# A three-layer fp32 network on one core: the scheduler's slacks, begin, look-ahead and transfer latency set to other values, and 28 leading idle transposes in place of 18

## The chip, the cores and the metric

The kernel runs on one core of one Trainium2 chip. The metric is the device time of one execution in microseconds. Before the change it is 800.46 us, the median of three runs (800.13 to 802.74 us). One more execution was profiled: it took 801.54 us, of which 799.8 us lie between its first and its last instruction. All rows below are of that execution.

Engines are named as in the profile: PE is the matrix engine (PEld its weight loads), DVE the vector engine, ACT the scalar engine, POOL the GpSimd engine, SP the engine that issues the DMAs.

## The reference

The program computes three layers in a row, all in fp32:

```python
# attention over a memory of 32 slots, 4 images x 8 heads, 576 positions, head size 64
a = exp(phi - max(phi, positions)); a = a / (sum(a, positions) + 1e-9)
k_m, v_m = einsum('bhsm,bhsd->bhmd', a, k), einsum('bhsm,bhsd->bhmd', a, v)
attn = softmax(q @ k_m^T / 8, slots)
x = (attn @ v_m) as 2304 tokens x 512
# layer 2
h = x @ w_in            # 512 -> 2048
g = maximum(0.01 * h, h)
x = g @ w_out           # 2048 -> 512
# layer 3
out = ((x @ w_a) * (x @ w_b)) @ w_out2   # 512 -> 1536, 1536 -> 512
```

## The kernel before, in words

**Arithmetic.** A product of two fp32 matrices is made of three passes of a faster number format: both factors are split into a high and a low part, and high x high, high x low and low x high are added up in PSUM (`PASSES`). The weights arrive as 64-bit words. Each weight tile is converted before use: two ACT operations (`high`, `low`, lines 460 and 463), then `clamp` (L467 on DVE, L392 on POOL), `shift` (L471), `join` (L475) and `add` (L478), and for most weights a copy to the high part (L405 on ACT, L407 on DVE) and a subtraction for the low part (L484 on DVE, L388 on POOL).

**Stages of the beginning.** For each image b and each half g of the heads, `kv_part` loads phi, k and v. It takes the maximum on DVE (L540) and the exponential on ACT (L541), transposes on PE (tiles `ta`, `tz`, L554 and L557) and copies the result back (`en`). PE multiplies it with k and v (tile `km`, L571), DVE normalises (`kvn`, L580), and PE transposes once more (`kvt`, L588). Two pairs of copies lead from there to `kd` and `vm`. `sc_both` then multiplies q with `kd` (tile `sc`, L632). `sc_part` is the softmax of these scores: on DVE a transpose (L654), the maximum (L662), the subtraction (L663), on ACT the exponential (L664), on DVE the sum and its reciprocal (L667 to L669), the product (L672) and a transpose back (L673). ACT copies the high part (`ahi`, L405), and DVE (L678) or POOL (L388) makes the low part (`alo`).

**Layer 2.** The values of the memory are first multiplied with `w_in` (`vw_unit`, L704; high and low part `vwh` and `vwl`, L714). `h_unit` (L757) then multiplies `ahi` and `alo` with `vwh` and `vwl`; `y_unit` (L796) multiplies the result `g` with `w_out`. There are four chunks of `w_in` and `w_out`, eight pieces of tokens (two for each image), and for each piece four blocks of h. Layer 3 (`ab_unit` L1008, `left_unit` L1062, `o_unit` L1102, `o_part` L1217) works through 12 chunks of its weights twice.

**What sets the order.** Nothing runs in the order in which the code is written. Each step is recorded as an `Op` with an engine (or several to choose from), a cost in microseconds and what it reads and writes. `Program.order` then plays the whole program through in a planned time and gives every step an engine, a place in that engine's queue and a buffer. Among the steps that are ready it takes the one with the earliest due time `o.late`. The due times come from `urgency`: the large matrix steps (those with a `pos`) have target times, which begin at `START` and add up their costs, and every other step is due so much earlier as its followers need, less its own `slack` from the table `SLACK`. `LEAD` says how many places ahead of the first one still missing a large matrix step may be taken. `LAT_DMA` is the planned delay between a transfer's end and its reader. The engines then execute their queues strictly in the order that came out.

SP's queue too is written in this order: it issues 323 transfers one after the other, and each begins when its buffer is free.

**Names in the change.** `warm` (L424) is the first work of PE: transposes of the identity matrix whose result nobody reads.

Of the kernel before, what the change touches and what calls it, by code (L numbers as in the profile page):

```python
# [52 lines left out]

PRE = 4
TURN = 0.15
SEVEN = 8
LEAD = 12
SLACK = {'phi0': 0.0, ('kv0', 0): 1.0, ('kv0', 1): 0.0, 'kvr0': 3.0, ('q0', 0): 0.0, ('q0', 1): 0.0, ('win0', 0): 5.37, ('win0', 1): 5.37, ('wout0', 0): 8.13, ('wout0', 1): 8.13, 'win': 4.9, 'wout': 4.64, 'wa': 23.6, 'wb': -0.15, 'wout2': 16.8, ('sc', 0, 0): 6.2, ('sc', 0, 1): 3.3, ('sc', 1, 0): 8.05, ('sc', 1, 1): 6.75, ('sc', 2, 0): 11.99, ('sc', 2, 1): 9.96, ('vw', 0, 0): 19.04, ('vw', 0, 1): 7.99, ('vw', 0, 2): 9.35, ('vw', 1, 0): -0.31, ('vw', 1, 1): 19.18, ('vw', 1, 2): 8.18}
START = 17.4
BIAS = 0.5  # L60
POOL_BIAS = 0.8
LAT, LAT_SAME, LAT_DMA = 0.4, 0.1, 1.0
OVER = {'PE': 0.0, 'ACT': 0.0, 'DVE': 0.0, 'POOL': 0.0, 'DMA': 0.0}
BLOCKED = 0.0
DMA_RATE, DMA_FIRST = 355e3, 0.0
SPARE = {'PE': 1.0, 'ACT': 1.03, 'DVE': 1.03, 'POOL': 1.03, 'DMA': 1.2}


# [20 lines left out]
def c_dma(nbytes):  # L89
    return max(0.6, nbytes / DMA_RATE)  # L90
# [15 lines left out]
class Program:  # L106
# [13 lines left out]
    def op(self, eng, cost, fn, r=(), w=(), tiles=(), pos=None, ahead=60.0, keep=0, slack=0.0, soon=False):  # L120
        o = Op()
        port = isinstance(eng, Port)
        o.costs = {e: (c - OVER[e]) * SPARE[e] for e, c in (eng if isinstance(eng, dict) else {eng: cost}).items()}
        eng = next(iter(o.costs))
        cost = o.costs[eng]
        o.eng, o.cost, o.fn, o.tiles, o.pos, o.seq, o.ahead, o.keep = eng, cost, fn, tuple(tiles), pos, len(self.ops), ahead, keep
        o.slack, o.soon = slack, soon
        o.port = port
        o.before, o.after = set(), []
        for x in r:  # L130
            if x in self.writer:
                o.before.add(self.writer[x])
        for x in w:
            if x in self.writer:
                o.before.add(self.writer[x])
            o.before.update(self.readers.pop(x, ()))
        for x in r:
            self.readers.setdefault(x, set()).add(o)
        for x in w:
            self.writer[x] = o  # L140
        o.before.discard(o)
        for x in o.before:
            x.after.append(o)
        self.ops.append(o)
        return o
# [20 lines left out]
    def order(self, target):  # L166
# [59 lines left out]
        while left:  # L226
# [5 lines left out]
            for e in ready:  # L232
                if at[e] > now + 1e-9:
                    continue
                for o in ready[e]:
                    if o.dep > now + 1e-9:
                        continue
                    if o.pos is not None and index[o.seq] > nth + LEAD:
                        continue
# [54 lines left out]
    def run(self, make, rounds=6):  # L294
        main = [o for o in self.ops if o.pos is not None]
        main.sort(key=lambda o: o.pos)
        target, t = {}, START
        for o in main:
# [35 lines left out]
def tile_mem_attention__leaky_mlp__bilinear_mlp(  # L334
# [29 lines left out]
    op, tile_of = pr.op, pr.tile  # L364
# [55 lines left out]
    tile_of(("warm",), "y", [P])  # L420

    def warm(T):
        for _ in range(18):
            nc.tensor.transpose(T["warm",], ident, ident)  # L424

    op("PE", 5.0, warm, tiles=[("warm",)], ahead=1e12)

# [11 lines left out]
    def weight(kind, c, k, after=()):  # L441
# [51 lines left out]
        op(Port({"DVE": 0.68}), 0, join, r=[raw], w=[a], tiles=[raw, cv], ahead=any_time)  # L493
        slack = SLACK[(kind + "0", k // 2) if first else kind]
        op(Port({"DVE": 0.62, "POOL": 2.45}), 0, add, r=[("l", key)], w=[a], tiles=[cv], ahead=any_time, slack=slack if kind == "win" else 0.0)
# [17 lines left out]
    def kv_part(b, g):  # L513
# [4 lines left out]
        if b == 0:  # L518
            tile_of(phi, "slot", [1, S])
            op("DMA", c_dma(P * S * 4), lambda T: nc.sync.dma_start(T[phi], phiT[b, :, g:g + 1, :]), w=[("e", b, g)], tiles=[phi], slack=SLACK["phi0"])  # L520
        elif g == 0:
# [9 lines left out]
        for i, k in enumerate(kvt):  # L531
            tile_of(k, "slot", [2, 512])
            op("DMA", c_dma(P * 4096), lambda T, i=i, k=k: nc.sync.dma_start(T[k], kv[b, g, :, 2 * i:2 * i + 2, :]), w=[k], tiles=[k], keep=6 if b else 0, slack=0 if b else SLACK["kv0", g])
        if g == 0:
            tile_of(rest, "slot", [2, 512], parts=64)
            op("DMA", c_dma(64 * 4096), lambda T: nc.sync.dma_start(T[rest], kv_rest[b]), w=[rest], tiles=[rest], keep=6 if b else 0, slack=0 if b else SLACK["kvr0"])

# [68 lines left out]
    def q_load(b, g):  # L606
# [5 lines left out]
        for x in range(2):  # L612
            q, cols = ("q", b, g, x), piece(x)
            n = cols.stop - cols.start
            tile_of(q, "slot", [2, n])
            op("DMA", c_dma(P * n * 8), lambda T, q=q, cols=cols: nc.sync.dma_start(T[q], qT[b, g, :, :, cols]), w=[q], tiles=[q], slack=SLACK["q0", x])

    def sc_both(b, x):
# [17 lines left out]

        op("PE", 4 * n / 2.4e3 + TURN, s_sc, r=[*qs, *(("kd", b % 2, g) for g in range(2))], w=scs, tiles=[*qs, *scs])
        for i in range(2):
            sc_part(b, i, x)

    def sc_part(b, g, x):
# [24 lines left out]
        def s_sum(T):  # L666
# [11 lines left out]
            lambda T, e: engines[e].tensor_tensor(T[alo][:, g, cols], T[at], T[ahi][:, g, cols].bitcast(F32), op=ALU.subtract),  # L678
            r=[at, kh], w=[kl], tiles=[at, ahi, alo], slack=SLACK["sc", min(b, 2), x],
        )  # L680
# [8 lines left out]
    def vw_unit(c, b, x, n):  # L689
# [9 lines left out]
        def prod(T):  # L699
# [6 lines left out]
        op(  # L706
            "PE", TURN + 4 * n / 2.4e3, prod, r=[("a", k[1:]) for k in ws] + [("vm", b, g) for g in range(2)], w=os, tiles=[*os, *ws],
            ahead=15.0,
# [364 lines left out]
    def by_seven(s, c):  # L1073
        return s == 1 and c < SEVEN

# [126 lines left out]
    def o_part(q, x, nth, pos):  # L1202
# [18 lines left out]
        def acc(i):  # L1221
            return ("osum", i)

        def part(T, i):
            return T[acc(i)][:, x, :]
# [12 lines left out]
        if q == 0:  # L1238
            op({"ACT": c_act(NB2), "DVE": c_dve(NB2)}, 0, lambda T, e: copy(e, part(T, i), T[o]), r=[o], w=[tok(i)], tiles=[o, acc(i)])
            return  # L1240
        last = q == SEVEN // 2 - 1
        op("DVE", 0.69, lambda T: nc.vector.tensor_tensor(part(T, i), T[o], part(T, i), op=ALU.add), r=[o], w=[tok(i)], tiles=[o, acc(i)])
# [116 lines left out]
```

## Time and profile before

| | us |
|---|---|
| median of three runs (lowest, highest) | 800.46 (800.13, 802.74) |
| the profiled execution | 801.54 |
| its span, first to last instruction | 799.8 |
| PE busy in the span | 775.5 (97%) |
| DVE, ACT, POOL busy | 615.9, 372.6, 119.9 |

[...] A row of a timeline gives start, duration, engine, line, operation, output and inputs, shape and number of the instructions that were merged into it. In brackets stands how long the engine was idle just before, and what it waited for.

### The profile page before, as it was taken

What the parts mean: (1) busy time and instruction counts of PE and PEld (TensorE: products, weight loads), DVE (VectorE), ACT (ScalarE), POOL (GpSimd) and SP (SyncE); (2) the same over time, 40 slices, a digit from 0 to 9 for tenths busy, and PEclk for the clock granted to TensorE, in tenths of its full rate; (3) what the DMA queues carried; (4) which work ended last, traced back from release to release, by engine and by line L of the source; (5) the groups of instructions that cost most, each with busy time, mean ns of one, the idle gap of its engine ahead of it and who ended that gap; (6) DMA issues with size and microseconds to landing.
All of it is one profiled execution on the core that took longest, in us unless ns stands there. A gap on an engine that the chain in (4) does not pass through costs nothing. (4 is left out here: it accounts for less than half of the span.)

```text
span 799.8 us, 12802 instructions
## 1 busy us (share of the span) xinstructions
PE 775.5 (97%) x4754; PEld 661.9 (83%) x4754; DVE 615.9 (77%) x1179; ACT 372.6 (47%) x810; POOL 119.9 (15%) x176
## 2 busy tenths in 40 slices
PE   6689999999999999999999999999999999999998
PEld 4367788989898889899988888888888888888886
DVE  5797798689868986676756988998864666798855
ACT  4557676757444754444435635444321154232210
POOL 0132051014003500010000302131210100024100
PEclk6679999999999999999999999999999999999999
DMA  9974211367143722033878854666487988777402
GB/s 331 387 233 143 91 70 54 99 203 246 46 145 111 273 65 79 1 107 109 304 262 306 277 190 167 227 206 212 166 286 287 310 267 286 233 229 239 150 1 105
DMA packets 56558, 149.99 MB, mean 188 GB/s; under 512 B 7216, under 2 KB 22576, under 8 KB 56496
## 3 DMA queue, kind: packets, MB, share of 16 engines
q1 hardware_dynamic: 56496, 149.18, 54.8%
q8 instruction: 37, 0.61, 0.3%
q14 instruction: 25, 0.20, 0.1%
HBM read 103.55 MB, written 45.61 MB: 187 GB/s over the span
## 5 line engine op out<-in xcount | busy, mean ns | idle before, releaser
L796 PE MATMUL y<-g,wout 128*128 128x320 f32 (+1 forms) x1152 | 216.1, 340 | 1.0 <-DVE wout L484 0.8
L796 PEld LDWEIGHTS y<-g,wout 128*128 128x128 f32 x1152 | 187.5, 190 | 23.1 <-issue 6.3
L1008 PE MATMUL abx<-yb_T,wo 128*128 128x512 f32 x432 | 110.2, 390 | 0.0
L1102 PE MATMUL o<-p,wout 128*128 128x512 f32 x384 | 94.9, 390 | 0.0
L1008 PEld LDWEIGHTS abx<-yb_T,wo 128*128 128x128 f32 x432 | 80.2, 188 | 16.1 <-ACT t L1019 0.2
L1019 ACT COPY t<-abx 128x512 f32<-128x512 f32 x72 | 42.1, 585 | 101.9 <-PE abx L1008 101.7
L722 ACT ACTIVATE g<-h 128x320 fp32r<-128x320 f32 (+1 forms) x128 | 52.5, 411 | 70.8 <-PE h L757 66.9
L1102 PEld LDWEIGHTS o<-p,wout 128*128 128x128 f32 x384 | 72.0, 188 | 15.3 <-DVE osum L1115 0.4
L757 PE MATMUL h<-ahi,vwh 128*128 128x320 f32 (+1 forms) x256 | 78.5, 307 | 2.7 <-ACT ahi L405 1.8
L757 PE MATMUL h<-alo,vwh 128*128 128x320 f32 (+1 forms) x256 | 76.6, 299 | 1.3 <-POOL alo L388 1.0
L757 PE MATMUL h<-ahi,vwl 128*128 128x320 f32 (+1 forms) x256 | 76.3, 298 | 0.0
L811 DVE TENSOR_TENSOR acc<-y,acc 128x320 f32<-128x320 f32 (+1 forms) x72 | 40.1, 556 | 36.7 <-PE y L796 36.3
L773 DVE TENSOR_TENSOR g<-t,g 128x256 fp32r<-128x256 f32 (+1 forms) x112 | 52.5, 473 | 17.8 <-ACT t L722 17.0
L757 PEld LDWEIGHTS h<-ahi,vwh 128*128 128x128 f32 x256 | 48.9, 191 | 11.6 <-issue 4.5
L722 ACT ACTIVATE t<-h 128x320 f32<-128x320 f32 (+1 forms) x128 | 52.3, 409 | 0.2
L757 PEld LDWEIGHTS h<-alo,vwh 128*128 128x128 f32 x256 | 49.0, 191 | 2.6 <-POOL alo L388 1.6
L757 PEld LDWEIGHTS h<-ahi,vwl 128*128 128x128 f32 x256 | 49.0, 191 | 0.0
L1016 DVE TENSOR_TENSOR t<-abz,t 128x512 f32<-128x512 f32 x48 | 33.0, 687 | 20.0 <-ACT t L1019 10.9
L1115 DVE TENSOR_TENSOR oacc<-o,oacc 128x512 f32<-128x512 f32 x40 | 27.5, 688 | 14.8 <-PE o L1102 13.9
L405 ACT CAST p<-t 128x512 fp32r<-128x512 f32 x31 | 19.2, 620 | 39.9 <-DVE t L1040 26.1
L1008 PE MATMUL abx<-yb_B,wo 128*128 128x512 f32 x144 | 36.9, 392 | 0.0
L1008 PE MATMUL abz<-yb_B,wo 128*128 128x512 f32 x144 | 36.7, 390 | 0.0
(311 smaller groups left out, 1348.2 us busy)
## 6 DMA issues: line engine op xcount, KB each, us to landing
k_wo<-wo SPq DMA_DIRECT2D x32, 512.0 KB, 5.0
wo<-k_wo SPq DMA_DIRECT2D x32, 512.0 KB, 4.6
raw_wout<-in_w_out_dram SPq DMA_DIRECT2D x24, 512.0 KB, 5.6
raw_win<-in_w_in_dram SPq DMA_DIRECT2D x16, 512.0 KB, 5.5
kv<-in_kv_dram SPq DMA_DIRECT2D x16, 512.0 KB, 10.6
k_yb_T<-yb_T SPq DMA_DIRECT2D x8, 512.0 KB, 7.2
raw_wa<-in_w_a_dram SPq DMA_DIRECT2D x8, 512.0 KB, 4.1
raw_wb<-in_w_b_dram SPq DMA_DIRECT2D x8, 512.0 KB, 4.6
```

Source lines behind the costliest of these rows:

```text
L405: nc.scalar.copy(dst, src)
L722: nc.scalar.activation(dst, src, AF.Prelu, alpha=0.01)
L757: nc.tensor.matmul(T[o], T[w[u]][:, k, fs], T[a[v]][:, k, cols], start=(k == 0 and i == 0), stop=(k == 1 and i == 2))
L773: lambda T, e: engines[e].tensor_tensor(T[g][:, i, 1, to], T[t], T[g][:, i, 0, to].bitcast(F32), op=ALU.subtract),
L796: nc.tensor.matmul(T[o], w[:, u, es], T[g][:, j, v, :], start=(f == 0 and p == 0), stop=(f == 3 and p == 2))
L811: "DVE", c_dve(m), lambda T: nc.vector.tensor_tensor(T[acc][:, i, :], T[o], T[acc][:, i, :], op=ALU.add),
L1008: nc.tensor.matmul(T[o], T[w][:, which, u, k * P:(k + 1) * P], T[ys[v]][:, k, :], start=first and k == 0 and x == 0, stop=k == 1 and x == ...
L1016: op("DVE", 0.69, lambda T: nc.vector.tensor_tensor(T[to], T[o], T[x], op=ALU.add), r=[o, x], w=[to], tiles=[o, x, to])
L1019: op("ACT", 0.59, lambda T: nc.scalar.copy(T[t], T[X]), r=[X], w=[t], tiles=[X, t])
L1102: nc.tensor.matmul(T[o], T[w][:, u, es], T[g][:, at, v, :], start=(x == 0 and k == 0), stop=(x == 1 and k == 2))
L1115: "DVE", c_dve(size), lambda T: nc.vector.tensor_tensor(T[acc][:, i, :], T[o], T[acc][:, i, :], op=ALU.add),
```

## The change

Only numbers change. The slacks are other ones for nearly every kind of step. `START` is 10.21 and not 17.4, so that all due times move forward against the transfers and conversions. `LEAD` is 9 and not 12, `LAT_DMA` 1.12 and not 1.0. The idle transposes are 28, and their planned cost is 0.28 us for each (7.84 us, before 5.0 us). Two names without effect (`DMA_FIRST`, the type of zeros in `OVER`) go too. The computation and the number of large matrix instructions stay the same.

```diff
+WARM = 28
-LEAD = 12
-SLACK = {'phi0': 0.0, ('kv0', 0): 1.0, ('kv0', 1): 0.0, 'kvr0': 3.0, ...
+LEAD = 9
+SLACK = {'phi0': -0.83, ('kv0', 0): 1.64, ('kv0', 1): -4.32, 'kvr0': 4.67, ...
-START = 17.4
+START = 10.21
-LAT, LAT_SAME, LAT_DMA = 0.4, 0.1, 1.0
+LAT, LAT_SAME, LAT_DMA = 0.4, 0.1, 1.12
...
-        for _ in range(18):
+        for _ in range(WARM):
             nc.tensor.transpose(T["warm",], ident, ident)

-    op("PE", 5.0, warm, tiles=[("warm",)], ahead=1e12)
+    op("PE", 0.28 * WARM, warm, tiles=[("warm",)], ahead=1e12)
```

The new lines are one further down: L588 is L589 in the changed program.

PE, image 0: the products `km` of both halves and the transposes `kvt` behind them. Before:

```order
L571 MATMUL km_0_189<-kvr_156,en_0_163 32x128 x4
L588 MATMUL kvt_0_221<-ident,kvn_0_217 128x128 x2
L571 MATMUL km_1_228<-kv_1_0_185,en_1_175 32x128 x8
L571 MATMUL km_1_228<-kv_1_1_211,en_1_175 32x128 x8
L571 MATMUL km_1_228<-kvr_156,en_1_175 32x128 x4
L588 MATMUL kvt_1_255<-ident,kvn_1_253 128x128 x2
```

and changed:

```order
L572 MATMUL km_0_197<-kvr_128,en_0_175 32x128 x4
L572 MATMUL km_1_233<-kv_1_0_192,en_1_180 32x128 x8
L572 MATMUL km_1_233<-kv_1_1_219,en_1_180 32x128 x8
L572 MATMUL km_1_233<-kvr_128,en_1_180 32x128 x4
L589 MATMUL kvt_0_256<-ident,kvn_0_229 128x128 x2
L589 MATMUL kvt_1_265<-ident,kvn_1_259 128x128 x2
```

The second `km` no longer stands behind the first `kvt`, which waits for DVE's `kvn`. Behind these rows, PE in both programs makes the first half of `vw` of image 0. Before, the second half and image 1's `ta` and `tz` follow and then the scores `sc` of image 0; now the scores come at once, then `ta` and `tz`, then the second half.

DVE, the softmax of image 0's first scores (`sm_0_0` and `sm_1_0` are its two halves, `mx` their maxima). Before:

```order
L407 COPY en_0_309<-ta_0_298 128x512
L714 TENSOR_TENSOR vwl_0_281<-vw_0_1_0_284,vwh_0_278 128x256
L714 TENSOR_TENSOR vwl_0_281<-vw_0_1_1_285,vwh_0_278 128x256
L467 TENSOR_SCALAR cv_wout_0_311<-cv_wout_0_311 128x512
L467 TENSOR_SCALAR cv_wout_1_315<-cv_wout_1_315 128x512
L467 TENSOR_SCALAR cv_wout_2_323<-cv_wout_2_323 128x512
L471 TENSOR_SCALAR cv_wout_0_311<-cv_wout_0_311 128x512
L471 TENSOR_SCALAR cv_wout_1_315<-cv_wout_1_315 128x512
L654 STREAM_TRANSPOSE sm_0_0_356<-sc_0_0_338 128x320
L654 STREAM_TRANSPOSE sm_1_0_359<-sc_1_0_339 128x320
L662 TENSOR_REDUCE mx_0_10_81<-sm_0_0_356 128x10
L662 TENSOR_REDUCE mx_0_10_83<-sm_1_0_359 128x10
```

and changed:

```order
L541 TENSOR_REDUCE kst_0_79<-phi_254 128x1
L541 TENSOR_REDUCE kst_1_80<-phi_254 128x1
L715 TENSOR_TENSOR vwl_0_291<-vw_0_0_0_275,vwh_0_288 128x256
L715 TENSOR_TENSOR vwl_0_291<-vw_0_0_1_276,vwh_0_288 128x256
L545 TENSOR_SCALAR kst_0_79<-kst_0_79 128x1
L546 RECIPROCAL kst_0_79<-kst_0_79 128x1
L655 STREAM_TRANSPOSE sm_0_0_315<-sc_0_0_294 128x320
L655 STREAM_TRANSPOSE sm_1_0_324<-sc_1_0_295 128x320
L663 TENSOR_REDUCE mx_0_10_81<-sm_0_0_315 128x10
L663 TENSOR_REDUCE mx_0_10_83<-sm_1_0_324 128x10
L664 TENSOR_TENSOR sm_0_0_315<-sm_0_0_315,mx_0_10_81 128x320
L664 TENSOR_TENSOR sm_1_0_324<-sm_1_0_324,mx_0_10_83 128x320
```

The softmax now stands ahead of all of DVE's work on the weight `w_out`, which moves behind it, and ahead of the second half of `vwl`. The two copies of `ta` to `en` of image 1 are ACT's now.

DVE, the end of that softmax (`at`) and the step to its low part `alo`. Before:

```order
L673 STREAM_TRANSPOSE at_0_0_387<-sm_0_0_356 128x320
L673 STREAM_TRANSPOSE at_1_0_412<-sm_1_0_359 128x320
L471 TENSOR_SCALAR cv_wout_3_348<-cv_wout_3_348 128x512
L475 SCALAR_TENSOR_TENSOR cv_wout_0_311<-raw_wout_0_258,cv_wout_0_311 128x512
L475 SCALAR_TENSOR_TENSOR cv_wout_1_315<-raw_wout_1_275,cv_wout_1_315 128x512
```

and changed:

```order
L674 STREAM_TRANSPOSE at_0_0_392<-sm_0_0_315 128x320
L674 STREAM_TRANSPOSE at_1_0_394<-sm_1_0_324 128x320
L472 TENSOR_SCALAR cv_wout_0_317<-cv_wout_0_317 128x512
L472 TENSOR_SCALAR cv_wout_1_326<-cv_wout_1_326 128x512
L679 TENSOR_TENSOR alo_403<-at_0_0_392,ahi_396 128x320
L679 TENSOR_TENSOR alo_403<-at_1_0_394,ahi_396 128x320
```

The two `alo` steps move from POOL to DVE. In exchange POOL takes two of the four `clamp` steps of `w_out`. On SP the one transfer that moves at the start is `kvr` (64 partitions, 256 KB): it stood seventh and stands first.

## Rows read from the trace of the kernel before

**Rows 1.** The page: busy time by engine, and the clock in 40 slices.

```profile
PE 775.5 (97%) x4754; PEld 661.9 (83%) x4754; DVE 615.9 (77%) x1179; ACT 372.6 (47%) x810; POOL 119.9 (15%) x176
...
PEclk6679999999999999999999999999999999999999
```

**Rows 2.** Stretches of the span: busy time of each engine, granted clock, DMA share, GB/s.

```profile
0.00:5.48 5.48, 3.71 (x18) 3.47 (x18) 0.00 (x0) 1.98 (x3) 0.70 (x6) 1.00 0.68 212
...
5.48:72.75 67.27, 50.40 (x517) 34.76 (x517) 55.36 (x138) 36.68 (x97) 14.33 (x19) 0.75 0.85 301
...
7.93:31.83 23.90, 17.62 (x176) 9.68 (x180) 16.43 (x44) 13.34 (x34) 0.00 (x0) 0.50 1.04 374
...
31.83:38.65 6.82, 3.04 (x68) 1.88 (x59) 6.68 (x19) 2.18 (x5) 1.35 (x2) 1.00 1.04 401
...
38.65:42.07 3.42, 2.97 (x12) 2.60 (x12) 3.42 (x6) 0.20 (x1) 0.78 (x1) 0.50 1.04 407
...
42.07:52.31 10.24, 8.01 (x62) 4.78 (x61) 9.71 (x20) 7.10 (x22) 6.41 (x8) 1.00 1.03 326
...
52.31:59.13 6.82, 6.11 (x33) 5.30 (x34) 6.58 (x19) 3.63 (x10) 1.47 (x2) 0.50 0.23 69
...
59.13:76.00 16.87, 15.53 (x200) 12.84 (x198) 13.21 (x40) 11.43 (x38) 5.04 (x7) 1.00 0.50 168
...
76.00:796.00 720.00, 718.48 (x4200) 621.36 (x4200) 556.90 (x1034) 330.86 (x700) 104.16 (x151) 1.00 0.52 177
```

**Rows 3.** PE's timeline: start, duration, what, idle before it and releaser.

```profile
1.36 3.71 PE L424 MATMUL warm<-ident 128*128 128x128 f32 x18 [1.36 <-POOL ident masks.py:199]
...
8.71 1.12 PE L554 MATMUL ta<-ident,phi 128*128 128x128 f32 x4 [3.65 <-ACT phi L541]
...
13.53 2.27 PE L571 MATMUL km<-kv,en 128*32 128x128 f32 x32 [2.17 <-DMA kv<-in_kv_dram]
...
20.74 0.69 PE L588 MATMUL kvt<-ident,kvn 128*128 128x128 f32 x2 [0.61 <-DVE kvn L580]
...
29.18 1.47 PE L632 MATMUL sc<-q,kd 64*32 64x320 f32 x16 [0.30 <-ACT en L405]
...
37.27 0.41 PE L757 MATMUL h<-ahi,vwh 128*128 128x320 f32 x1 [1.85 <-ACT ahi L405]
...
49.93 1.69 PE L796 MATMUL y<-g,wout 128*128 128x320 f32 x7 [0.84 <-DVE wout L484]
...
72.47 0.44 PE L588 MATMUL kvt<-ident,kvn 128*128 128x128 f32 x2 [0.97 <-DVE vwl L714]
```

**Rows 4.** DVE's timeline, instructions that waited, and two rows of L475.

```profile
12.74 1.29 DVE L475 SCALAR_TENSOR_TENSOR cv_win<-raw_win,cv_win 128x512 int32<-128x512 int32 x2
...
16.45 0.48 DVE L580 TENSOR_SCALAR kvn<-km,kst 128x256 f32<-128x256 f32 x1 [0.70 <-PE km L571]
...
18.17 0.46 DVE L407 COPY kd<-kvt 64x64 f32<-64x64 f32 x2 [1.24 <-ACT vm L405]
...
20.20 0.48 DVE L580 TENSOR_SCALAR kvn<-km,kst 128x256 f32<-128x256 f32 x1 [1.57 <-PE km L571]
...
26.53 0.69 DVE L407 COPY en<-ta 128x512 f32<-128x512 f32 x1 [0.92 <-PE ta L554]
...
30.75 0.91 DVE L654 STREAM_TRANSPOSE sm<-sc 128x320 f32<-128x320 f32 x2 [1.20 <-PE sc L632]
...
37.34 3.84 DVE L475 SCALAR_TENSOR_TENSOR cv_wout<-raw_wout,cv_wout 128x512 int32<-128x512 int32 x4
...
62.96 0.43 DVE L678 TENSOR_TENSOR alo<-at,ahi 128x256 fp32r<-128x256 f32 x1 [1.49 <-ACT ahi L405]
...
66.64 0.92 DVE L654 STREAM_TRANSPOSE sm<-sc 128x320 f32<-128x320 f32 x2 [1.23 <-PE sc L632]
```

**Rows 5.** POOL's timeline: the two steps `alo` of image 0, and one whole `clamp`.

```profile
37.30 2.13 POOL L388 TENSOR_TENSOR alo<-at,ahi 128x320 fp32r<-128x320 f32 x2 [35.99 <-ACT ahi L405]
...
117.49 2.52 POOL L392 TENSOR_SCALAR cv_wout<-cv_wout 128x128 f32<-128x128 f32 x4 [1.45 <-ACT cv_wout L460]
```

More of the change, by code (lines that the diff above doesn't have):

```diff
@@ L55 @@
 TURN = 0.15
+WARM = 28
 SEVEN = 8
-LEAD = 12
-SLACK = {'phi0': 0.0, ('kv0', 0): 1.0, ('kv0', 1): 0.0, 'kvr0': 3.0, ('q0', 0): 0.0, ('q0', 1): 0.0, ('win0', 0): 5.37, ('win0', 1): 5.37, ('wout0', 0): 8.13, ('wout0', 1): 8.13, 'win': 4.9, 'wout': 4.64, 'wa': 23.6, 'wb': -0.15, 'wout2': 16.8, ('sc', 0, 0): 6.2, ('sc', 0, 1): 3.3, ('sc', 1, 0): 8.05, ('sc', 1, 1): 6.75, ('sc', 2, 0): 11.99, ('sc', 2, 1): 9.96, ('vw', 0, 0): 19.04, ('vw', 0, 1): 7.99, ('vw', 0, 2): 9.35, ('vw', 1, 0): -0.31, ('vw', 1, 1): 19.18, ('vw', 1, 2): 8.18}
-START = 17.4
+LEAD = 9
+SLACK = {'phi0': -0.83, ('kv0', 0): 1.64, ('kv0', 1): -4.32, 'kvr0': 4.67, ('q0', 0): 0.8, ('q0', 1): 0.5, ('win0', 0): 3.41, ('win0', 1): 3.67, ('wout0', 0): 8.83, ('wout0', 1): 8.29, 'win': 5.47, 'wout': 4.48, 'wa': 26.21, 'wb': -1.48, 'wout2': 15.22, ('sc', 0, 0): 10.3, ('sc', 0, 1): 3.3, ('sc', 1, 0): 8.05, ('sc', 1, 1): 7.33, ('sc', 2, 0): 12.17, ('sc', 2, 1): 10.91, ('vw', 0, 0): 17.13, ('vw', 0, 1): 8.31, ('vw', 0, 2): 10.0, ('vw', 1, 0): 5.69, ('vw', 1, 1): 17.51, ('vw', 1, 2): 8.21}
+START = 10.21
 BIAS = 0.5
 POOL_BIAS = 0.8
-LAT, LAT_SAME, LAT_DMA = 0.4, 0.1, 1.0
-OVER = {'PE': 0.0, 'ACT': 0.0, 'DVE': 0.0, 'POOL': 0.0, 'DMA': 0.0}
+LAT, LAT_SAME, LAT_DMA = 0.4, 0.1, 1.12
+OVER = {'PE': 0.0, 'ACT': 0, 'DVE': 0, 'POOL': 0.0, 'DMA': 0.0}
 BLOCKED = 0.0
-DMA_RATE, DMA_FIRST = 355e3, 0.0
+DMA_RATE = 355000.0
 SPARE = {'PE': 1.0, 'ACT': 1.03, 'DVE': 1.03, 'POOL': 1.03, 'DMA': 1.2}
```

## The prediction

> **What bounds the kernel now.** I read the page first. PE is busy for 775.5 us of the span, 97%, and its clock is below full only in the first two of the 40 slices [rows 1]. So whatever an order can still save lies at the very beginning, unless the new order spoils the rest. Then the table of stretches shows how sharp the border is: from 76 to 796 us PE is busy for 718.48 of 720.00 us at a granted clock of 1.00, so it waits for 1.52 us in all [rows 2]. There is almost nothing to win there, and much to lose. Before 76 us it is different: between 5.48 and 72.75 us PE is busy for 50.40 of 67.27 us, and the clock was at half for a good part of it.
>
> PE's timeline then says who it waits for: ACT's exponential, the DMA of `kv`, and from then on DVE again and again, or ACT on a chain that begins at DVE (`kvn`, `ahi`, `wout`), last at 72.47 us, where `kvt` of image 2 waits 0.97 us for `vwl` [rows 3]. I call this place M. It is a good border: PE, in both programs, has made the same matrix instructions up to it, and has the same left behind it. So the question is when M comes.
>
> DVE is busy for 55.36 of the 67.27 us up to 72.75 [rows 2]. The other 11.91 us are gaps. Its timeline has 9.60 us of them in eight waits: 0.70 and 1.57 us for `km`, twice about 1.25 us (one is shown) for the copy `vm`, 0.92 us for `ta`, 1.20 us for `sc`, 1.49 us for `ahi`, 1.23 us for the next `sc` [rows 4]. What is left, 2.31 us, is small gaps. DVE comes to M last, so its ledger gives M: 5.48 us until its first instruction, 55.36 us of work, 11.91 us of gaps.
>
> **The change part by part.**
>
> *The idle transposes.* 18 took 3.71 us from 1.36 us on, so 28 take 5.77 us and end at 7.13 us; the first `ta` starts at 8.71 us after 3.65 us of idleness [rows 3]. They lie inside this wait and cost nothing as long as the exponential comes no sooner than 7.13 us, and with `kvr` ahead of it it comes later. They may keep the clock up a little longer. It fell in the stretch that begins at 7.93 us [rows 2]; if `ta` ran at full speed, that would save some 0.56 of its 1.12 us, behind which the `kv` transfer is waited for all the same. I take zero.
>
> *The transfer `kvr`, now first.* Its 256 KB delay `phi` by 0.70 us at the 374 GB/s of the stretch from 7.93 us on, by 1.24 us at the 212 GB/s of the beginning [rows 2]. I take 1.0 us, by which DVE begins later. `km` starts when `kv` has landed [rows 3], with the same bytes ahead of it in both orders, so it does not move; the 0.70 us that DVE waited for it has less to wait for.
>
> *Both `km` in a row, the `kvt` behind them, the scores at once.* Before, DVE went twice through the chain `kvn`, `kvt`, `vm`, `kd` and waited in each (0.70 and 1.24, then 1.57 and 1.25 us). With both halves together it goes through once, and the work of one half lies in the wait of the other. I keep one wait of 1.25 us and half of 1.57 us, so 2.04 us. The wait of 0.92 us for `ta` goes because ACT makes these copies now. The 1.20 us before the softmax goes because `sc` comes earlier against DVE's work: the second `km` needs three transfers of 512 KB more after the first began at 13.53 us, 4.2 us at 374 GB/s, and ends near 18.4 us; from `kvn` to the end of `kd` took 2.18 us (16.45 to 18.63) [rows 4], one more pair 0.94 us, `sc` 1.47 us [rows 3]: it ends near 23.0 us, not 30.65 us. DVE has the conversion of `w_in` and half of `vwl` to do until then.
>
> *What remains.* The two late waits, 1.49 and 1.23 us, belong to image 1 and come again: 2.72 us. Of the small gaps I keep half, 1.16 us. Together 2.04 + 2.72 + 1.16 = 5.92 us of gaps, not 11.91.
>
> *DVE's work up to M.* It gains two `alo`, two subtractions and four copies, and loses two copies of `ta`, two of the `clamp` steps of `wout` and some casts: some 4.4 us against 4.5 us, so zero. One thing is not in this count. Four L475 took 3.84 us while POOL made `alo` beside them; two alone took 1.29 us, so four would take 2.58 us [rows 4, 5]. These 1.26 us go with the `alo`. In their place POOL makes two `clamp` steps, 2.52 us each [rows 5], beside the softmax. If DVE lost there in the same share (1.26 in 2.13 us), that is 2.98 us; at the other end it loses nothing. I take 1.26 us again, so a net of zero, with 1.7 us to one side and 1.3 us to the other. [...]
>
> *The sum.* 5.48 + 1.0 + 55.36 + 5.92 = 67.76 us, against 72.75 us: M comes 5.0 us sooner. PE must be there too. Between its first `h` (37.27 us) and M it needs 35.20 us [rows 3]; the softmax moves by at least as much as the ledger, so `h` starts at 32.3 us at the latest and PE is at M by 67.5 us: it waits no more for its own work. With gaps of only 2 us M comes 8.9 us sooner; with gaps of 7.5 us, 3.4 us.
>
> *The clock.* It fell twice after PE had been half idle: at 38.65 us after 3.04 busy of 6.82 us, and at 52.31 us after 8.01 of 10.24 us. The first stretch of 3.42 us at 0.50 had the work of 1.71 us at full speed [rows 2]. Such stretches ahead of M cost nothing while DVE is last there. Behind M each costs 1.71 us, and PE has more waiting ahead of M than it had; I give one such stretch a chance of one half, 0.9 us. [...]
>
> Behind M the work is the same, and I take PE's 1.52 us of waiting as it was. So the profiled execution of 801.54 us (a span of 799.8 and 1.74 us around it) becomes 801.54 - 5.0 + 0.9 = 797.4 us. It stood 1.08 us above the median of 800.46, so the median becomes **796.4 us**.
>
> **The rivals.**
>
> *DVE stays the bound behind M.* Image 2 and 3 repeat the chain, and DVE is busy for 13.21 of 16.87 us from 59.13 to 76 us, where PE waits 1.34 us [rows 2]. If all comes 5 us sooner, the transfers and DVE's work for these images have not become faster. Between those 1.34 us once more and the 3.66 us that DVE had free there, 2.5 us are given back: 798.9 us. For it: the wait at M for `vwl`. Against it: 718.48 of 720.00 us right behind.
>
> *The clock falls again behind M.* Two or three stretches at half speed, 3.4 or 5.1 us in place of the 0.9: 798.9 or 800.6 us, in the middle 799.7. For it: the two falls. Against it: from 59.13 us on the clock held at 1.00 although PE waited [rows 2].
>
> *Waits in the full stretch (slower).* A large matrix step may now be taken only 9 places ahead, not 12, and the conversions are due at other times. From 76 us on a `clamp`, `shift` or transfer that comes late stops PE, since nothing else stands in its queue. Seven waits as long as the 0.97 us at M [rows 3] cost 6.8 us: 803.2 us. It decides from 4.1 us of new waits on, and shows as slower from 6.5 us on. Against it: DVE is busy for only 556.90 of these 720 us, POOL for 104.16.
>
> *The gaps go nearly altogether.* With 2.0 us left the ledger gives 8.9 us less and 0.9 us for the clock: 792.5 us. Against it: the late waits of image 1 are on the chain of the next image's softmax, which did not change its place.
>
> *The change does less than it says.* If the transposes are all that counts, nothing moves, since they end inside a wait. The order is another one in fact, so this has no chance of its own.
>
> **How the numbers follow.** Forecast 0.50, DVE behind M 0.17, clock 0.15, waits in the full stretch 0.08, gaps gone 0.10. About 0.3%, 2.4 us, is what a measurement of this kernel can tell from no change: faster is below 798.06, slower above 802.86 us. The forecast's own range is 794.0 to 798.0 us (a gain of 3.4 us with the 0.9 us gives 798.0). Faster: 0.48 of it, all of the gaps' 0.10, 0.05 and 0.04 of the first two rivals: 0.67. Slower: 0.06 of the full stretch, 0.02 of the clock: 0.08. The same: 0.25. The range from 792.2 to 801.0 us leaves out some 0.06 below (gaps below 2 us) and 0.10 above (the full stretch and the worst of the clock).
>
> **What would show it.** The idle transposes end near 7 us and `ta` starts near 9.7 us. The second `km` ends near 18.4, the first `sc` near 23, the first `h` starts between 29 and 32.3 us. DVE's gaps up to M are near 6 us, with no wait for `ta`, and the L475 of `wout` take some 0.65 us each. M comes near 68 us, released by DVE. Behind it PE is busy for all but 1.5 to 3 us at a clock of 1.00. The forecast is wrong if M comes after 70 us, if PE itself comes to M last, or if PE waits for more than 4 us between M and the end.

## The result, and the profile after

The changed kernel takes 791.74 us (median of 4 runs, 790.76 to 793.23) against 800.30 us before (4 runs): a ratio of 0.9889, 95% interval 0.9861 to 0.9916. Measured once more beside later runs it took 792.14 us (5 runs) against 800.26 us, a ratio of 0.9897 (0.9884 to 0.9911). So it is 8.6 us faster in the first measurement and 8.1 us in the second, where 4.1 us were forecast; the time lies below the stated range, which began at 792.2 us.

The profiled execution took 793.23 us with a span of 791.5 us, 8.3 us less than the profiled one before. The page of the changed kernel, engine totals and clock:

```profile
PE 773.7 (98%) x4764; PEld 661.8 (84%) x4764; DVE 618.7 (78%) x1182; ACT 372.2 (47%) x800; POOL 119.8 (15%) x173
...
PEclk7599999999999999999999999999999999999999
```

The totals hardly differ from [rows 1]; the idle time of PE does. The stretches of the changed kernel, up to M and from M to PE's last instruction (behind each busy time the number of its instructions, the clock as a share of full speed):

```profile
0.00:6.39 6.39, 5.00 (x28) 4.76 (x28) 0.00 (x0) 1.99 (x3) 0.70 (x6) 1.00 0.68 203
6.39:67.16 60.77, 48.33 (x514) 32.93 (x515) 53.95 (x140) 37.49 (x98) 18.38 (x22) 0.75 0.97 344
67.16:787.53 720.37, 720.37 (x4222) 624.07 (x4222) 564.09 (x1042) 332.77 (x701) 100.70 (x145) 1.00 0.51 177
```

and the last of these stretches in the kernel before:

```profile
72.47:795.83 723.36, 721.64 (x4222) 623.95 (x4222) 560.09 (x1041) 334.24 (x713) 105.17 (x153) 1.00 0.52 177
```

The same 4222 matrix instructions follow M. M comes at 67.16 us and not 72.47 (5.31 us sooner), and the rest takes 720.37 and not 723.36 us (2.99 us less): together 8.30 us, the whole difference. Behind M, PE now is busy without a gap; before it was idle for 1.72 us there.

PE's timeline of the changed kernel, the places of [rows 3]:

```profile
1.36 5.00 PE L425 MATMUL warm<-ident 128*128 128x128 f32 x28 [1.36 <-POOL ident masks.py:199]
10.16 1.12 PE L555 MATMUL ta<-ident,phi 128*128 128x128 f32 x4 [3.81 <-ACT phi L542]
13.28 2.26 PE L572 MATMUL km<-kv,en 128*32 128x128 f32 x32 [0.65 <-DMA kv<-in_kv_dram]
18.08 0.65 PE L572 MATMUL km<-kvr,en 64*32 64x128 f32 x8
19.93 0.69 PE L589 MATMUL kvt<-ident,kvn 128*128 128x128 f32 x2 [0.58 <-DVE kvn L581]
23.53 1.31 PE L633 MATMUL sc<-q,kd 64*32 64x320 f32 x14 [0.61 <-DVE vwl L715]
32.22 0.63 PE L758 MATMUL h<-ahi,vwh 128*128 128x320 f32 x1 [3.35 <-ACT ahi L406]
47.03 3.03 PE L797 MATMUL y<-g,wout 128*128 128x320 f32 x12
67.16 0.41 PE L589 MATMUL kvt<-ident,kvn 128*128 128x128 f32 x2 [1.43 <-DVE vwl L715]
```

The second `km` ends at 18.73 us (18.4 forecast), the scores end at 24.84 us (23.0), the first `h` starts at 32.22 us (29 to 32.3), and at M PE waits for DVE's `vwl`, 1.43 us, as forecast. DVE's waits in the changed kernel, and two of its L476:

```profile
19.39 0.48 DVE L581 TENSOR_SCALAR kvn<-km,kst 128x256 f32<-128x256 f32 x1 [1.42 <-PE kvt L589]
21.12 0.46 DVE L408 COPY kd<-kvt 64x64 f32<-64x64 f32 x2 [0.81 <-ACT vm L406]
24.95 0.91 DVE L655 STREAM_TRANSPOSE sm<-sc 128x320 f32<-128x320 f32 x2 [0.88 <-PE sc L633]
34.11 1.28 DVE L476 SCALAR_TENSOR_TENSOR cv_wout<-raw_wout,cv_wout 128x512 int32<-128x512 int32 x2
41.62 1.29 DVE L485 TENSOR_TENSOR wout<-cv_wout,wout 128x512 fp32r<-128x512 f32 x2 [0.88 <-ACT wout L406]
```

The ledger: 6.39 us until the first instruction, 53.95 us of work, 6.82 us of gaps. The forecast had 6.48, 55.36 and 5.92 (counted up to 72.75 us, 0.28 us past M). The two late waits of image 1 [rows 4] are not there.

### The profile page after: what moved, and what is told of

It reads as the page before. It is cut to its first block, busy times and chain, and to the rows that moved or that the text cites. A ratio compares the mean times of both kernels' runs of the same rounds, so it can differ in the third digit from the quotient of the medians.

```text
span 791.5 us, 12795 instructions
## 1 busy us (share of the span) xinstructions
PE 773.7 (98%) x4764; PEld 661.8 (84%) x4764; DVE 618.7 (78%) x1182; ACT 372.2 (47%) x800; POOL 119.8 (15%) x173
## 4 chain that ended last, share of the span: by engine, by line
PE 96%; DVE 1%; DMA 1%; SPq 1%; issue 0%; ACT 0%
PE y L797 26%; PE abx L1009 17%; PE h L758 13%; PE o L1103 13%; PE abz L1009 8%; PE os L1218 5%; PE aby L1009 4%; PE b L1063 2%; PE a L1063 2%; PE vw L705 2%; PE km L572 2%; DMA kv<-in_kv_dram 1%; PE sc L633 1%; PE ta L555 0%; PE kvt L589 0%; SPq L455 0%
## 5 line engine op out<-in xcount | busy, mean ns | idle before, releaser
L797 PE MATMUL y<-g,wout 128*128 128x320 f32 (+1 forms) x1152 | 213.2, 338 | 0.0
L774 DVE TENSOR_TENSOR g<-t,g 128x256 fp32r<-128x256 f32 (+1 forms) x101 | 47.7, 487 | 14.3 <-ACT t L723 12.1
L389 POOL TENSOR_TENSOR g<-t,g 128x256 fp32r<-128x256 f32 (+1 forms) x27 | 25.5, 959 | 109.3 <-ACT t L723 87.2
```

The lines of the kernel that those rows point to most:

```text
L774: lambda T, e: engines[e].tensor_tensor(T[g][:, i, 1, to], T[t], T[g][:, i, 0, to].bitcast(F32), op=ALU.subtract),
L797: nc.tensor.matmul(T[o], w[:, u, es], T[g][:, j, v, :], start=(f == 0 and p == 0), stop=(f == 3 and p == 2))
```

## The experiments

All profiles in one table. The median is that of all executions of a row; M and what stands to its right are read from one profiled execution. "Listed" is PE's idle time between M and its last instruction.

| kernel | median (lowest, highest) | M | M to PE's end | listed |
|---|---|---|---|---|
| before | 800.30 (799.77, 802.74) | 72.47 | 723.36 | 1.72 |
| changed | 791.74 (790.76, 793.23) | 67.16 | 720.37 | 0 |
| changed, 18 transposes | 792.65 (791.72, 793.33) | 65.19 | 720.81 | 0 |
| before, 28 transposes | 801.93 (798.49, 803.39) | 71.02 | 725.11 | 2.57 |
| changed start, old numbers behind | 792.97 (792.51, 794.23) | 64.56 | 722.23 | 0.98 |
| old start, new numbers behind | 798.07 (797.09, 798.88) | 71.06 | 721.13 | 0.37 |
| changed, `kvr` seventh | 793.29 (790.75, 794.17) | 64.56 | 720.47 | 0 |
| changed, `km` apart | 794.49 (794.06, 795.22) | 67.95 | 720.41 | 0 |
| changed, scores late | 798.07 (796.48, 799.10) | 70.39 | 720.45 | 0 |
| before, `k_wo` sooner | 799.16 (798.04, 800.74) | 71.13 | 722.27 | 0.80 |
| changed, again | 792.14 (791.91, 793.00) | 66.82 | 720.45 | 0 |
| changed, 42 transposes | 792.50 (791.97, 793.34) | 65.99 | 720.44 | 0 |
| the same and 11 more | 791.42 (790.60, 792.03) | 65.52 | 720.41 | 0 |
| changed, `clamp` on DVE | 792.91 (791.58, 794.46) | 65.95 | 720.38 | 0 |

The kernel before took 800.94 us (23 runs) beside rows three to six, 800.73 (19) beside the next four, 800.26 (9) beside the last four.

**The idle transposes.** In the changed kernel and in the one before, only the number is changed:

```diff
-        for _ in range(WARM):
+        for _ in range(18):
```

> The changed kernel with 18 idle transposes in place of 28; the order of all engines stays the changed one. Theory (the order brings the gain: DVE comes to M 5.3 us sooner, PE's waits behind M go): the transposes lie inside the wait for the exponential, M stays at 67.2 us within 0.3 us, and the time within 1.5 us of the changed kernel's 791.7 us. Rival (the transposes keep the clock up at the beginning and so bring part of the gain): ta and the first km run at half speed for longer, M comes 1.5 us later or more, and the time is 793.5 us or more.

> The kernel before with 28 idle transposes, its order as it was. Theory: nothing changes, 800.3 us within 1.5 us, M at 72.5 us. Rival (the transposes bring part of the gain): M comes at 71 us or sooner, and the time is 798.5 us or less.

The changed order with 18 takes 792.65 us; the old order with 28 has a ratio of 1.0008 (0.9992 to 1.0024) to the kernel before. So the number of transposes has no effect that can be told from the noise. Both M came sooner than expected, though, by 2.0 and 1.5 us, with the same order of every engine; the second lies at the edge of the rival's 71 us, but its time does not. What goes with this is told below, in the part on why the prediction was wrong. And in the second, the 1.5 us did not reach the end: from M on it took 725.11 us.

**Start and rest apart.** Both sets of numbers are planned, and in the final pass the planner goes over from the one to the other when 18 large matrix steps are placed. In the traces PE, DVE, ACT and POOL leave the order of the start 7 to 25 us behind M:

```diff
+            if mixed and not turned and nth >= SWITCH:
+                turned = True
+                use(1 - FIRST)
...
+                for o in self.ops:
+                    o.late = o.lates[1 - FIRST] + shift
```

> The changed order of all engines up to a little behind M, and behind it an order drawn by the old numbers (slacks, look-ahead, transfer latency). Theory: M at 67.2 us as in the changed kernel; behind it PE waits again, since the old numbers leave waits, 1 to 4 us of them: the time is 792.5 to 796 us. Rival (the waits behind M go because all comes sooner from the beginning): PE waits for less than 0.5 us behind M, as in the changed kernel, and the time is 791 to 792.3 us.

> The old order of all engines, with 18 transposes, up to a little behind M, and behind it an order drawn by the new numbers. Theory: M at 72.5 us as before; behind it PE hardly waits, so some 3 us of the gain remain: 796.5 to 798 us. Rival (the start alone brings it): PE's waits behind M are as before, 1.7 us listed, and the time is 800 us within 1 us.

The old start with new numbers behind it takes 798.07 us, 2.9 us below the 800.94 us beside it: this is the part of the gain behind M, alone (ratio 0.9967, 0.9955 to 0.9979). Of the 0.37 us listed there 0.29 us still lie in the old order's part, at 74.56 us. The changed start with the old numbers behind it has PE wait again behind M (0.98 us listed, 1.86 us longer than in the changed kernel), though its M came sooner than in the changed kernel. So the waits did not go because all came sooner; they went with the numbers that order the rest. The result with the changed start rests on one profile: its time, 792.97 us, can't be told from the changed kernel's. Which of the numbers does it (slacks, look-ahead or transfer latency) no run separates. The old numbers, drawn anew behind another start, leave fewer waits than the old order itself has, so the two parts don't add up to the whole.

**One wait behind M.** In the kernel before with 28 transposes, PE lost 1.52 us at 648.60 us. PE's and DVE's rows there:

```profile
648.60 1.42 PE L1217 MATMUL os<-pb_T,w 128*128 128x512 f32 x5 [1.52 <-DVE pb_T L1181]
```

```profile
642.53 0.68 DVE L1181 TENSOR_TENSOR pb_B<-pf,pb_B 128x512 fp32r<-128x512 f32 x1
647.51 0.43 DVE L407 CAST pb_T<-pf 128x512 fp32r<-128x512 f32 x1 [4.30 <-DMA k_wo<-wo]
```

and in the execution of the kernel before from which the prediction was made:

```profile
647.62 0.43 DVE L407 CAST pb_T<-pf 128x512 fp32r<-128x512 f32 x1 [2.52 <-DMA k_wo<-wo]
```

DVE may write `pb_T` only when the transfer `k_wo` has emptied its buffer, and this landed at 647.5 us in both, though M came 1.45 us sooner in the one with 28 transposes and the step ahead of `pb_T` 1.9 us sooner. So a gain at the beginning was lost here. The transfer too was issued sooner there, at 638.21 and not 640.09 us; 15 of its 16 parts had landed by 645.96 us, and the last came at 647.42 us. Why this part was late, and whether it is late in every execution of the old order, the profiles don't show. The experiment takes that one transfer three loads forward:

```diff
+        move([2309], 2311)   # k_wo of chunk 11, piece 1, behind that of piece 3
```

> The kernel before, its order as it was, but one transfer near 640 us, the store k_wo whose buffer the step pb_T of L407 takes over at 647.6 us, is issued three loads sooner. Theory (in the old order this store holds PE up whenever the work before it comes early, so a gain ahead of it is lost there; 1.52 us listed in one execution of the old order, none in another): DVE's wait of 2.5 to 4.3 us for it goes, the median falls by 0.5 to 1.5 us to 799.4 to 800.4 us, and no run lies above 802.5 us. Rival (the spread of the old order has another source): the median and the highest run stay, 800.9 and 803 us or more.

The median fell by 1.6 us to 799.16 us and the highest run to 800.74 us, beside 804.18 us before. This is what the theory expected, a little more of it; but the ratio, 0.9984, has an interval that reaches no change (0.9967 to 1.0000), so the gain is likely and not shown. DVE's row there now has no wait:

```profile
642.01 0.42 DVE L418 CAST pb_T<-pf 128x512 fp32r<-128x512 f32 x1
```

**The parts of the start, undone one at a time** in the finished changed order. `move` puts steps behind another one in the list of all steps:

```diff
+        move([4], 305)    # kvr behind the fourth raw_win
+        move([29], 14)    # second km behind the first kvt
+        move([68, 69, 78, 70, 79, 71, 80, 72, 81, 73, 82], 321)   # sc and softmax behind vwl
```

> The changed order of every engine, but the transfer kvr of image 0 issued seventh again, not first. Theory (its place is nearly neutral, since kv and phi have the same bytes ahead of them in sum): DVE begins about 1 us sooner (5.5 us), both km start as they did (13.3 and 16.1 us), M within 1 us of 65 to 67 us, the time 791 to 793 us. Rival (kvr first is what lets both km run in a row): the first km starts 0.7 us later or more and M comes 1 to 2 us later, 793.5 us or more.

> The changed order, but on PE the second km of image 0 stands behind the first kvt again. Theory (km in a row saves a turn of the chain): the second km starts at 18.6 us, not 16.1, when kvn and the first kvt are done, the second kvt and the scores come 2 us later, DVE has 1 to 2 us more of gaps there, M comes 1 to 2 us later and the time is 793.5 to 794.5 us. Rival (DVE has work that fills the gap): M within 0.5 us, 791.5 to 793 us.

> The changed order, but the first scores sc of image 0 stand on PE behind image 1's ta and tz and the second half of vw again, and the first softmax on DVE (and its exponential on ACT) behind the second half of vwl. Theory (early scores are the largest part of M's gain): DVE waits 2 us more for sc, the first h comes 3 us later, M 2 to 3.5 us later, the time is 794 to 796 us. Rival (the softmax is not on the chain to M): the first h comes later, but M stays within 1 us and the time below 793.5 us.

For `kvr` no cost can be told from the noise: its profile has as early an M as any, but its median, 793.29 us, lies just above the expected 791 to 793 us. The second `km` behind the first `kvt` costs 2.4 us against the 792.14 us of the changed kernel in a later measurement, the upper end of what was expected; all four runs are slower than all nine of the changed kernel:

```profile
18.14 0.69 PE L600 MATMUL kvt<-ident,kvn 128*128 128x128 f32 x2 [1.88 <-DVE kvn L592]
18.75 1.94 PE L583 MATMUL km<-kv,en 128*32 128x128 f32 x32
21.88 0.69 PE L600 MATMUL kvt<-ident,kvn 128*128 128x128 f32 x2 [0.61 <-DVE kvn L592]
```

The late scores cost 5.9 us: 798.07 us, where 794 to 796 us were expected. M came 3.2 to 3.6 us later than in the two profiles of the changed kernel, in an execution of 796.54 us, one of the fastest of its ten; where the slower ones lost the rest no profile shows. PE's rows with them:

```profile
23.17 1.06 PE L566 MATMUL ta<-ident,phi 128*128 128x128 f32 x8 [2.14 <-ACT phi L553]
28.09 1.64 PE L644 MATMUL sc<-q,kd 64*32 64x320 f32 x16 [0.97 <-DVE vwl L726]
35.91 0.63 PE L769 MATMUL h<-ahi,vwh 128*128 128x320 f32 x1 [6.18 <-ACT ahi L417]
```

The scores then wait on PE behind `ta`, which waits 2.14 us for image 1's exponential, and PE is idle for 6.18 us ahead of `h`: I had counted the moved work, not the waits of the work that it is put behind. Of the parts undone here, the early scores bring the most ahead of M. The two costs are no shares of one sum, since each was undone with the other in place.

**The clock ahead of M.** The changed kernel again, then 42 transposes, which leave 1.70 us of the wait for the first exponential, and then 11 more in the wait ahead of the first `h`:

```diff
+            if o.seq == 317:
+                self.fill()   # 11 idle transposes behind the second half of vw
```

> The changed kernel itself, as it is, beside the next three. Theory (its time varies by some 2.5 us with the clock granted ahead of M): runs between 790.5 and 793.5 us, those with the higher mean clock being the faster; no waits of PE behind M in the profile, 720.4 us from M to PE's end within 0.3 us. Rival (the waits behind M had gone by chance): M to PE's end takes 721.5 us or more in this profile.

> The changed order with 42 idle transposes, not 28, which last until about 9.5 us, nearly to the first ta at 10.2 us. Theory (half speed ahead of the first km costs time in the changed order): the clock stays at 1.00 until ta, M comes at 64.6 us more often, and the median falls by 0.5 to 1.5 us against the changed kernel beside it. Rival (the clock at the beginning costs nothing, as in the old order): the median within 0.5 us of it.

> The same with 42, and 11 more idle transposes on PE behind the second half of vw of image 0, in the wait of 3.4 us for ahi ahead of the first h. Theory: the clock does not fall there either, h and y of image 0 run at full speed, M at 64.5 us or sooner, the median 1 to 2 us below the changed kernel's. Rival (PE ahead of M is hidden behind DVE whatever its clock): the median within 0.5 us of the changed kernel's, or above it where the 11 transposes delay the first h.

42 transposes bring nothing. With 11 more the median is 0.7 us lower than the changed kernel's, but their intervals against the kernel before overlap (0.9874 to 0.9903, and 0.9884 to 0.9911), so whether it beats the changed kernel is unclear. The clock did fall in both all the same: from 20 to 32 us it was 0.50 with 42, and 0.72 with 11 more. That the runs of the changed kernel are ordered by their mean clock was expected and is wrong: 793.00 us at 0.985, but 791.91 us at 0.983.

**POOL beside the softmax.**

```diff
+        for n in (355, 364):
+            by[n] = (by[n][0], "DVE")
+        move([355, 364], 321)
```

> The changed order, but the two clamp steps of wout that POOL makes in 4.9 us beside the first softmax are DVE's, two instructions of 0.37 us each behind the second half of vwl. Theory (POOL beside the softmax costs DVE little: 1.3 us was allowed for): DVE's instructions between 25 and 30 us become shorter by less than 0.6 us in sum, the two new ones cost 0.75 us, M within 0.7 us, the time within 1 us of the changed kernel's. Rival (DVE loses 2.98 us there, the upper bound): M comes 2 us sooner and the time falls by 1.5 us or more.

792.91 us, M at 65.95 us. With POOL's `clamp` beside it, DVE's subtraction (two L664) took 0.97 us, without it 0.88 us; two small steps (L669) 0.27 and 0.23 us, without it 0.17 us each. In sum 0.25 us, not the 1.26 us that I took. The median is 0.8 us above the changed kernel's 792.14 us, and M 0.9 to 1.2 us sooner than in its two profiles; both are within what these vary by.

## Why the prediction was wrong

**The step that failed** is the last of the sum: "Behind M the work is the same, and I take PE's 1.52 us of waiting as it was", with 0.9 us more for the clock. Behind M 2.99 us went, and no stretch at half speed came. Of the 4.2 us between the forecast of the profiled execution (797.4 us) and its measured time (793.23 us), 3.9 us lie here and 0.3 us at M. Three things were missed.

First, the new numbers order the whole program, and I had looked for harm behind M but not for gain, since only 1.52 us of idle time were to be seen. The old start with new numbers behind it shows the gain alone.

Second, a wait costs more than the idle time that the trace lists. The kernel before, around the longer one of two waits for L722:

```profile
275.35 0.28 PE L757 MATMUL h<-alo,vwh 128*128 128x256 f32 x1
275.47 0.28 PE L757 MATMUL h<-ahi,vwl 128*128 128x256 f32 x1
276.28 0.39 PE L757 MATMUL h<-ahi,vwh 128*128 128x256 f32 x1 [0.53 <-ACT t L722]
276.50 0.28 PE L757 MATMUL h<-alo,vwh 128*128 128x256 f32 x1
```

These instructions overlap and start 0.12 us apart. Around the wait they start 0.81 and 0.22 us apart, so 0.79 us are lost where 0.53 are listed: until the next one starts again, the end of the last one counts as busy. In the table, 1.72 us listed go with 2.99 us (723.36 - 720.37), 2.57 with 4.7, 0.98 with 1.86 and 0.80 with 1.9 us: 1.7 to 2.4 times as much. Counted over all 4222 starts, against the usual distance (the median) of each pair of shapes, the starts were late by 15.6 us in sum before and by 12.5 us in the changed kernel, while the usual distances add up to 709.0 and 709.1 us. So the 2.99 us are starts that came late, and not matrix instructions that became shorter.

Third, the old order has a transfer that landed at 647.5 us in both of its profiles, also where the rest came sooner. It cost nothing in the execution that I read, and 1.52 us in the other. A wait that is off the path by little does not show as a wait of PE; DVE's 2.52 us for a DMA at a place where DVE had nothing else to do was in the trace to be seen.

**What was right, and why less than it seems.** M came 5.3 us sooner, 5.0 were forecast, for the reasons given: DVE was last at M, its gaps fell from 11.91 to 6.82 us, and the wait for `ta` went. But the terms of the gaps were off and cancelled. The early ones are about 4.0 us and not 2.04 (1.42 for `kvn`, 0.81 for `kd`, 0.88 for `sc`, and 0.84 in two waits at the very start). What is left was taken as 1.16 us and is 2.87, with a new wait of 0.88 us for `wout`. And the late waits of 2.72 us, which I let come again, were not part of the order: the same old order shows 0.16 us there with new numbers behind M,

```profile
65.24 0.91 DVE L699 STREAM_TRANSPOSE sm<-sc 128x320 f32<-128x320 f32 x2 [0.16 <-PE sc L677]
```

and M then came at 71.02 to 71.13 us in three profiles. They came with the half speed of 52.31 to 59.13 us [rows 2] in one execution. PE's products with `w_out` there, in the kernel before (granted clock 0.50) and with 28 transposes (1.00):

```profile
54.05 6.07 PE L796 MATMUL y<-g,wout 128*128 128x320 f32 x24
53.87 3.78 PE L796 MATMUL y<-g,wout 128*128 128x320 f32 x24
```

So "such stretches ahead of M cost nothing while DVE is last there" was wrong: DVE waits for PE ahead of M, and a slow PE makes M late, by 1.4 us there. Of the 5.3 us between the two M, then, 1.4 us belong to that execution and not to the old order. In the changed order M lies between 64.56 and 67.16 us. At 64.56 us the second `km` ends at full speed and the chain goes on so (granted clock 1.00 from 19.05 to 25.87 us, 0.50 there in the changed kernel's first profile); the rows of the changed order with `kvr` seventh, against 0.65 and 0.69 us above:

```profile
18.06 0.42 PE L583 MATMUL km<-kvr,en 64*32 64x128 f32 x8
18.42 0.44 PE L600 MATMUL kvt<-ident,kvn 128*128 128x128 f32 x2
```

Two profiles of the changed order in which the first `ta` starts at the same time (11.07 us with 18 transposes, 11.06 us in the changed kernel again) differ in the same way (clock 1.00 and 0.50 from 19.05 to 25.87 us), and their M by 1.63 us (65.19 and 66.82 us):

```profile
18.84 0.42 PE L572 MATMUL km<-kvr,en 64*32 64x128 f32 x8
18.92 0.65 PE L572 MATMUL km<-kvr,en 64*32 64x128 f32 x8
```

The clock is not all that varies: the first `ta` of the changed kernel started at 10.16 us in one profile and at 11.06 us in the other. What would decide the clock there was not found; two attempts to hold it changed little.

**The rivals.** DVE did not remain the bound behind M, and the clock did not fall again there. The slower case had its place right (waits in the full stretch, from other numbers) and its sign wrong: the old numbers had these waits. That the gaps go nearly altogether did not happen; its 792.5 us came near the measured time by luck. The transposes were free, as taken (28 took 5.00 us, not 5.77). Two readings of the rows were wrong without weight for the sum: the clock is below full in three slices of the page, not two [rows 1], and PE was not half idle before the fall at 52.31 us but busy for 8.01 of 10.24 us [rows 2].

**POOL and DVE.** By these rows the exchange of `alo` for `clamp` was a gain of about 1 us and not zero: the slow L475 [rows 4] went (two now take 1.28 us) and the `clamp` steps cost DVE 0.25 us. DVE's work up to M fell by 1.13 us, to 53.95 us from 55.08 us (the stretch up to 72.47 us). No run has `alo` back on POOL alone, so this part is worked out and not tested. Now POOL is the slow one beside the same steps of DVE:

```profile
35.75 3.44 POOL L389 TENSOR_TENSOR g<-t,g 128x320 fp32r<-128x320 f32 x1 [5.84 <-ACT t L723]
```

Three such steps at 43.56 us took 2.69 us. Before, POOL's `alo` began at 37.30 us and the L475 at 37.34 us [rows 4, 5], and DVE was slow (3.84 us for four); in the changed kernel DVE's row of steps had begun at 34.11 us, POOL's step began at 35.75 us, and POOL was slow. What decides which of the two is slow was not shown. Here the loser was mostly the engine that nobody waited for, though not alone: of the four L479 behind these steps, three took 0.68 us and one, at 38.65 us, 1.09 us.

## What to carry to other kernels

When a planner's numbers change, the whole order changes: compare the stretches on both sides of a place where both programs have done the same work, and look for gains in the full part too. Price a wait of PE from the starts of the instructions around it, not from the listed idle time (0.79 us were lost here where 0.53 were listed). Before a wait in one profile is taken for a property of the order, look whether it lies in a stretch at half speed (2.72 us of late waits came with one here), and look for transfers that land just in time: they can eat what is gained ahead of them (1.52 us at 648.60 us here).

## What the runs showed that was not expected

The granted clock in the records can be missing. The profile of the old start with new numbers behind it has 1.00 in every stretch, as in

```profile
7.93:26.00 18.07, 12.68 (x128) 6.73 (x129) 12.41 (x33) 7.94 (x22) 0.00 (x0) 1.00 1.03 373
```

but its matrix instructions there took as long as those of the kernel before at 0.50 (the same eight, at 15.73 us, 0.65 us):

```profile
16.02 0.65 PE L616 MATMUL km<-kvr,en 64*32 64x128 f32 x8
```

Eight of these take 0.42 us at 1.00 (in the kernel before at 33.63 us). The length of a known instruction is the better witness, and runs can't be sorted by their mean clock.
